# A transformer block: the attention gate applied to finished sums on GpSimd instead of to the output projection's weights, its columns made on VectorE, and the first half's LayerNorm moved to other steps

## The chip, the cores and the metric

The kernel runs on one core of a Trainium2 chip. The core has five engines, which run side by side and meet at semaphores: TensorE (PE in the profile; PEld is its weight load), VectorE (DVE), ScalarE (ACT), GpSimd (POOL) and SyncE (SP, which here only issues DMAs, in the order written). The metric is the device time of one execution in microseconds (us). Three runs of the kernel before took 1762.35, 1762.66 and 1764.65 us; the median is 1762.66 us.

## The reference

The block has 2048 rows of width 512. A condition vector `c` gives six vectors of 512: shift, scale and gate for the attention, and the same for the feed-forward part.

```python
x = A_x
mod = (_silu(c) @ w_mod).reshape(c.shape[0], 6, 1, -1)
sa, ca, ga, sb, cb, gb = (mod[:, 0], mod[:, 1], mod[:, 2], mod[:, 3], mod[:, 4], mod[:, 5])
h = _layernorm(x, axis=-1) * (1 + ca) + sa
x = x + ga * _A_ref(h, A_k_cache, A_v_cache, A_wq, A_wo)
h = _layernorm(x, axis=-1) * (1 + cb) + sb
x = x + gb * _B_ref(h, B_w_gate, B_w_up, B_w_down)
```

`_A_ref` projects `h` with `wq` to 32 query heads of 128, attends for each to 512 cached keys and values (8 key-value heads, four query heads on each), and projects the joined heads with `wo` back to 512. `_B_ref` is `(gelu(h @ w_gate) * (h @ w_up)) @ w_down` with an inner width of 1792. The change concerns `ga`: the gate multiplies the columns of the attention's output, so it may multiply the columns of `wo` beforehand, or the finished sum afterwards.

## The kernel before

**Numbers.** TensorE multiplies 16-bit floats. Every operand is kept as a high and a low half (`t[:, 0]` and `t[:, 1]`, made by `halves`, L152, or `split_post`, L673), and a product is three matmuls (`mm3`, L85 to L88: high by high, high by low, low by high). So that the halves use their range, each weight is multiplied by a scale found from its own sum of squares: ScalarE squares and sums, TensorE adds over partitions, VectorE and GpSimd turn that into a scale and its reciprocal (`norm2`, and the `..._spread` functions).

**Halves and units.** The 2048 rows are 16 tiles of 128. Tiles 0 to 7 are the first half, 8 to 15 the second. In each half, 16 pairs of heads run one after another, and each pair makes four units (two heads by two blocks of 512 rows). A unit is four score tiles; the main loop's counter `t` counts score tiles, 512 in all, and one value of `t` is called a *step* here. In a step TensorE computes one score tile `ps` (three matmuls) and up to three pieces of other work from a queue (query projection, products of probabilities and values `po`, output projection `py`), some 2.6 us in all. VectorE takes the row maximum `nm`, ScalarE the exponential `ee` and the scaled high half of the probabilities `p`, VectorE their low half, and SP issues a transposing DMA of `p` to `pt`. There are two `ps` banks, so the score matmuls of step t+2 wait for the exponential of step t.

**Order.** All order is written by hand. `at(t, f)` puts work behind the pieces of step t, `at(("w", t), f)` behind that, and `at(("d", t), f)` between the maximum and the low half. `sched` lists a load and the steps of its use, and issues the load some steps ahead; `within` issues a load between two steps when SP has no other. Each engine runs its instructions strictly in the order in which they were written. The steps repeat with period 16: even steps hold more VectorE work (a half of a query or output tile, an accumulation) than odd ones.

**Weights.** In the first half every weight is read in 32 bits, scaled, split, used, and stored as halves in `KEPT`; the second half reads them from there. For `wo`, `wo_items` (L570) loads a row tile twice: once for its sum of squares, once to be multiplied, at L584, by a row `gs`, the gate's row times the scale `osc`, and split. `o_spread` (L277) makes `osc` from the sums and `gam`, the greatest absolute value of the gate's row.

**The gate.** Four tiles of `w_mod` are loaded (`gate_load`), and TensorE multiplies them by the activated condition in steps 6 to 9 (`gate_cols`, through `early_cols`, L947), each of the four calls 4 matmuls of 128x128 weights in 32 bits on one column. `mod_row(2)` in step 11 spreads the column over partitions by four transpositions, and ScalarE copies it to `rows[2]`. The other vectors come from `mod_col` (L133): one VectorE instruction, multiply and accumulate, for a tile of `w_mod`.

**Sums.** `acc[ti]` is a row tile's sum in SBUF, of 8 buffers. It is loaded with `x`, and every second pair of heads `y_tasks` (L871) adds a projection result to it (L883). After the last pair `attn_final` (L889) stores it to `y1[ti]` and, three steps later, loads the tile that takes the buffer next.

**LayerNorm.** Rows of the second half's queries are normalised during the first half, two tiles at a time, by `ln_pair` at positions that `plan_pair` takes from `PLAN[1]`; those for the feed-forward part in the second half from `PLAN[2]`. Per pair VectorE has two groups of statistics (L381 to L385) and four wide instructions `xs` (L473, L471), GpSimd four subtractions of half tiles (L479) and four low halves `turn` (L492), ScalarE four high halves, and SP the loads and four transposing DMAs.

**Feed-forward.** Its weights are prepared on GpSimd during the second half (`prep_set`, `prep_wd`; L1341 multiplies a tile of `w_down` by the second gate's row times a scale). After step 512 only matmuls and the gelu remain, product by product: `f_at(q, k, f)` puts work behind product k of set q. The first half's `acc` is reloaded and the second half's rows get their LayerNorm there.

## Time and profile before

The profiled execution took 1763.88 us; its span, first instruction to last, is 1762.1 us.

| what | us |
|---|---|
| median of three runs | 1762.66 |
| profiled execution | 1763.88 |
| its span | 1762.1 |
| TensorE busy | 1724.3 |
| VectorE busy | 1455.9 |
| ScalarE busy | 1207.7 |
| GpSimd busy | 896.2 |
| mean granted TensorE clock | 0.999 of full speed |

Attention runs from about 25 us (step 0) to about 1350 us, the feed-forward part behind it; the first half ends near 690 us. In the rows of a profile L12 is line 12 of the kernel; `a<-b` is a tile written from a tile read, with buffer numbers left out; `x512` counts instructions. A row of groups has the busy time in us and the mean of one instruction in ns, and behind the second bar the engine's idle time before them with the work that ended it. A row of waits has who waited for whom, then total us, times, and the longest. A row of windows has the stretch in us, then busy us and number of instructions for PE, PEld, DVE, ACT and POOL, the granted clock, the share of the DMA engines and GB/s. A row of a timeline has the start and the length in us. Matmuls overlap in the pipeline: one has 379 ns, but they follow each other every 0.216 us.

### The profile page before, as it was taken

How to read it: one execution, taken by the hardware profiler on the slowest of the kernel's cores; microseconds unless marked ns; L12 is line 12 of the kernel's file. 1: busy time of each engine (PE TensorE's matmuls, PEld its weight loads, DVE VectorE, ACT ScalarE, POOL GpSimd, SP SyncE). 2: the span in 40 equal slices, each digit the busy share in tenths (PEclk: the TensorE clock that was granted, in tenths of full speed). 3: DMA queues.
4: the chain of work that ended last, by engine and by line, in shares of the span. 5: the costliest groups of instructions: out<-in, count | busy, mean ns of one | idle time of the engine just before them, and what ended most of it. 6: DMA issues, size and time to landing. Idle time of an engine off the chain costs nothing.

```text
span 1762.1 us, 25746 instructions
## 1 busy us (share of the span) xinstructions
PE 1724.3 (98%) x8034; PEld 787.8 (45%) x8034; DVE 1455.9 (83%) x2541; ACT 1207.7 (69%) x2716; POOL 896.2 (51%) x1113
## 2 busy tenths in 40 slices
PE   8899999999999999999999999999999999999999
PEld 5444444444444444444444444444444444444444
DVE  7888898989898889888888897988875788676666
ACT  6888877777777877778878778788774344434333
POOL 4879878887888773216666667666300233000000
PEclk9999999999999999999999999999999999999999
DMA  7999999999998998999999999999976545252222
GB/s 233 215 195 212 207 213 202 220 199 220 209 213 195 225 203 163 204 214 218 220 214 220 233 223 206 227 224 216 201 143 140 168 127 134 81 200 75 87 75 75
DMA packets 691690, 328.14 MB, mean 186 GB/s; under 512 B 596960, under 2 KB 607456, under 8 KB 691552
## 3 DMA queue, kind: packets, MB, share of 16 engines
q1 hardware_dynamic: 691264, 325.97, 81.0%
q8 instruction: 63, 1.03, 0.2%
q14 instruction: 75, 0.61, 0.1%
q10 hardware_dynamic: 288, 0.52, 0.1%
HBM read 127.54 MB, written 53.61 MB: 103 GB/s over the span
## 4 chain that ended last, share of the span: by engine, by line
PE 77%; POOL 8%; DVE 7%; ACT 4%; issue 2%; DMA 1%; SPq 0%; POOLq 0%; ACTq 0%
PE py L88 8%; PE py L86 8%; PE py L87 8%; PE ps L86 5%; PE ps L88 5%; PE ps L87 5%; PE po L86 5%; PE po L88 5%; PE po L87 5%; PE fa L86 3%; PE fa L88 3%; PE fa L87 3%; PE qa L86 2%; PE qa L88 2%; PE qa L87 2%
## 5 line engine op out<-in xcount | busy, mean ns | idle before, releaser
L915 ACT ACTIVATE ee<-ps,nm 128x512 f32<-128x512 f32 x512 | 350.1, 684 | 265.5 <-DVE nm L906 263.6
L934 DVE SCALAR_TENSOR_TENSOR p<-ee,rr,p 128x512 f16<-128x512 f32 x512 | 452.8, 884 | 1.8 <-ACT p L929 1.5
L906 DVE TENSOR_REDUCE nm<-ps 128x1 f32<-128x512 f32 x512 | 349.9, 683 | 97.3 <-PE ps L88 95.1
L929 ACT ACTIVATE p<-ee,rr 128x512 f16<-128x512 f32 x512 | 363.1, 709 | 8.8 <-DMA pt<-p 8.0
L86 PE MATMUL ps<-k,qt 128*128 128x512 f16 x512 | 193.8, 379 | 20.9 <-ACT ee L915 20.2
L86 PE MATMUL po<-pt,v 128*128 128x512 f16 x512 | 194.1, 379 | 1.6 <-DVE p L934 0.8
L88 PE MATMUL ps<-k,qt 128*128 128x512 f16 x512 | 194.1, 379 | 1.3 <-DVE qt L675 1.3
L87 PE MATMUL py<-wo,ot 128*128 128x512 f16 x512 | 194.0, 379 | 0.0
L88 PE MATMUL py<-wo,ot 128*128 128x512 f16 x512 | 194.0, 379 | 0.0
L88 PE MATMUL po<-pt,v 128*128 128x512 f16 x512 | 194.0, 379 | 0.0
L87 PE MATMUL po<-pt,v 128*128 128x512 f16 x512 | 194.0, 379 | 0.0
L86 PE MATMUL py<-wo,ot 128*128 128x512 f16 x512 | 194.0, 379 | 0.0
L87 PE MATMUL ps<-k,qt 128*128 128x512 f16 x512 | 193.9, 379 | 0.0
L391 POOL TENSOR_TENSOR rs<-rs,nhalf 128x1 f32<-128x1 f32 x32 | 23.4, 731 | 227.4 <-DVE rs L385 224.6
L675 DVE SCALAR_TENSOR_TENSOR ot<-po,ot 128x512 f16<-128x512 f32 x128 | 87.0, 680 | 39.5 <-ACT ot L674 39.3
L87 PEld LDWEIGHTS <-w 128*128 128x128 f16 x728 | 71.3, 98 | 87.0 <-issue 1.7
L88 PEld LDWEIGHTS <-w 128*128 128x128 f16 x728 | 71.3, 98 | 86.6 <-issue 0.8
L86 PEld LDWEIGHTS <-w 128*128 128x128 f16 x728 | 71.2, 98 | 86.7 <-DMA w<-kept 1.3
L883 DVE SCALAR_TENSOR_TENSOR acc<-py,ysc,acc 128x512 f32<-128x512 f32 x128 | 94.5, 738 | 10.9 <-PE py L88 10.9
L883 DVE SCALAR_TENSOR_TENSOR acc<-py,dysc,acc 128x512 f32<-128x512 f32 x112 | 81.3, 744 | 26.4 <-PE py L88 26.2
L915 ACT ACTIVATION_READ_ACCUMULATOR ee<-ps,nm 128x1 f32 x512 | 99.4, 194 | 0.0
L86 PE MATMUL py<-wo,at 128*128 128x512 f16 x224 | 84.9, 379 | 0.0
(269 smaller groups left out, 3760.6 us busy)
## 6 DMA issues: line engine op xcount, KB each, us to landing
w<-kept SPq DMA_DIRECT2D x123, 256.0 KB, 3.3
wo<-kept SPq DMA_DIRECT2D x60, 256.0 KB, 3.5
raw<-in_wo SPq DMA_DIRECT2D x56, 256.0 KB, 3.1
kept<-stage SPq DMA_DIRECT2D x56, 256.0 KB, 3.1
kept<-w SPq DMA_DIRECT2D x39, 256.0 KB, 3.2
rw<-in_wq SPq DMA_DIRECT2D x38, 256.0 KB, 3.2
pt<-p SPq DMA_TRANSPOSE x512, 3.4
kept<-wo SPq DMA_DIRECT2D x32, 256.0 KB, 2.7
```

The source lines that it names most:

```text
L86: nc.tensor.matmul(ps, lhi, rhi, start=first, stop=False, skip_group_check=chain)
L87: nc.tensor.matmul(ps, lhi, rlo, start=False, stop=False, skip_group_check=chain)
L88: nc.tensor.matmul(ps, llo, rhi, start=False, stop=last, skip_group_check=chain)
L391: nc.gpsimd.tensor_tensor(st["rs"], st["rs"], nhalf, op=ALU.pow)
L675: return lambda: nc.vector.scalar_tensor_tensor(t[:, 1, :], src, scale, t[:, 0, :], op0=ALU.mult, op1=ALU.subtract)
L883: nc.vector.scalar_tensor_tensor(acc[ti], st["p"], by, acc[ti], op0=ALU.mult, op1=ALU.add)
L906: nc.vector.tensor_reduce(nm, E[t]["ps"], axis=AX.X, op=ALU.max, negate=True)
L915: nc.scalar.activation(e, E[t]["ps"], AF.Exp, bias=E[t]["nm"], scale=1.0, accum_out=sm[:, t % 2:t % 2 + 1])
L929: nc.scalar.activation(p16[:, 0, :], E[t]["e"], AF.Copy, scale=E[t]["r"])
L934: nc.vector.scalar_tensor_tensor(p16[:, 1, :], E[t]["e"], E[t]["r"], p16[:, 0, :], op0=ALU.mult, op1=ALU.subtract)
```

## The change

The weights of `wo` are multiplied by their scale alone (one GpSimd instruction with a scalar in place of one with two tensors, and no row `gs`). The sum starts afresh from the first projection instead of from `x` (`fresh`), and when it is finished GpSimd multiplies it by the gate's row and adds `x`, which is loaded once more as `xr`. For tiles 0 to 7 this takes place one and three steps after the last accumulation, with the store six steps after; for tiles 8 to 15 at once, with the stores and reloads at listed places of the feed-forward part. The gate's columns come from `mod_col` at steps 207 to 221, its row at step 224. The second gate's row and scale are applied to `w_down` by two instructions per tile, without `gs`. The first two LayerNorm plans become one, a step or two earlier; the third moves six positions later. The `ln` buffers grow from two to three.

```diff
 def mod_row(j):
-        rows[j] = pool.tile([P, D], F32, tag="gate", name="gate", bufs=1)
+        rows[j] = pool.tile([P, D], F32, tag=f"gate{j}", name="gate", bufs=1)
         nc.scalar.activation(rows[j], ps, AF.Copy)
-        absmax(col("gam", j // 3), rows[j])
+        if j == 5:
+            absmax(col("gam", 1), rows[j])
 def o_spread(qd, m):
-        norm2(w, m, 4, 1.0)
-        pool_ts(w, w, col("gam", 0), 1.0 / TOP14)
-        pool_ts(w, w, 1e-30, 1.0, ALU.max)
+        norm2(w, m, 4, 1.0 / TOP14)
...
-            X[k] = pool.tile([P, D], F32, tag="ln", name="xs", bufs=2)
+            X[k] = pool.tile([P, D], F32, tag="ln", name="xs", bufs=3)
...
             def parts(sp=sp, h=h):
-                nc.gpsimd.tensor_tensor(sp["r"], sp["r"], m["g"], op=ALU.mult)
+                times(sp["r"], col("osc", qd))
...
-        def more():
-            m["g"] = pool.tile([P, D], F32, tag="gs", name="gs", bufs=1)
-            pool_ts(m["g"], rows[2], col("osc", qd))
...
+            if fresh:
+                acc[ti] = pool.tile([P, D], F32, tag="acc", name="acc", bufs=2 * QT)
+                ts(acc[ti], st["p"], by)
+            else:
+                nc.vector.scalar_tensor_tensor(acc[ti], st["p"], by, acc[ti], op0=ALU.mult, op1=ALU.add)
...
+    def residual(ti):
+        XR[ti] = pool.tile([P, D], F32, tag="ln", name="xr", bufs=3) if ti < 2 * QT + 3 else raw("xr")
+        dma(XR[ti], rows_of(x, ti))
+    def gate(ti):
+        nc.gpsimd.tensor_tensor(acc[ti], acc[ti], rows[2], op=ALU.mult)
+    def back(ti):
+        nc.gpsimd.tensor_tensor(acc[ti], acc[ti], XR[ti], op=ALU.add)
+    def keep_row(ti):
         y1[ti] = dram.tile([P, D], F32, name=f"y{ti}")
         dma(y1[ti], acc[ti])
-        nxt = (ti + 2 * QT) % NT
-        at(now[0] + 3, lambda: load_acc(nxt, rows_of(x, nxt) if ti < 2 * QT else y1[nxt]))
+    def attn_final(ti):
+        if ti < 2 * QT:
+            residual(ti)
+            at(("w", now[0] + 1), lambda: gate(ti))
+            at(("w", now[0] + 3), lambda: back(ti))
+            at(now[0] + 6, lambda: keep_row(ti))
+        else:
+            gate(ti)
+            back(ti)
...
-    for dt in range(KT):
-        sched(6 + dt, (lambda dt=dt: gate_load(dt), [lambda dt=dt: gate_cols(dt)]), ahead=8)
-    at(("d", 10), lambda: ts(cols[:, 2, :], gps["ps"][:, 0:KT], 1.0, None, ALU.mult))
-    for j, ts_ in ((3, (239, 243, 247, 251)), (4, (241, 245, 249, 253)), (5, (274, 278, 282, 286))):
+    for j, ts_ in ((2, (207, 211, 215, 221)), (3, (239, 243, 247, 251)), (4, (241, 245, 249, 253)), (5, (274, 278, 282, 286))):
...
-    at(11, lambda: mod_row(2))
+    at(224, lambda: mod_row(2))
+    for i in range(2 * QT):
+        at(T - 10 + i, lambda i=i: residual(2 * QT + i))
...
-    PLAN = {1: (-6, 0, 2, 4, -1, 6, 8, 16, 20, 21, ((8, 9, 12), (18, 19, 22), (24, 25, 28), (28, 29, 33))),
-            2: (-6, 0, 2, 5, 8, 14, 16, 18, 21, 22, ((7, 8, 11), (19, 20, 23), (25, 26, 29), (31, 32, 35)))}
+    PLAN = (-6, 0, 2, 4, 0, 6, 10, 16, 19, 20, ((7, 8, 12), (17, 18, 22), (23, 24, 28), (27, 28, 32)))
...
-        plan_pair(1, 78 + 32 * i, i, lambda k, i=i: rows_of(x, 2 * QT + QT * k + i))
-        plan_pair(2, 287 + 48 * i, i, lambda k, i=i: y1[QT * k + i])
+        plan_pair(1, 77 + 32 * i, i, lambda k, i=i: rows_of(x, 2 * QT + QT * k + i))
+        plan_pair(2, 285 + 48 * i, i, lambda k, i=i: y1[QT * k + i])
...
         def make(k):
-            nc.gpsimd.tensor_tensor(st[k], st[k], m["g"], op=ALU.mult)
+            nc.gpsimd.tensor_tensor(st[k], st[k], rows[5], op=ALU.mult)
+            times(st[k], col("dsc", n))
...
-        b = 20 + 16 * i
+        b = 26 + 16 * i
...
+    for i, ((a, b), (c, d)) in enumerate(zip(((1, 3), (1, 3), (1, 4), (1, 5), (2, 0), (2, 1), (2, 3), (2, 5)),
+                                             ((1, 5), (1, 6), (2, 1), (2, 2), (2, 4), (2, 5), (3, 0), (3, 2)))):
+        f_at(a, b, lambda i=i: keep_row(2 * QT + i))
+        f_at(c, d, lambda i=i: load_acc(i, y1[i]))
```

The first place is VectorE in steps 118 to 120 of the first half (a step begins with `nm`; `qt` and `ot` are query and output halves, `p` the probabilities, `xs` a LayerNorm tile). Before:

```order
L906 TENSOR_REDUCE nm<-ps 128x1
L925 RECIPROCAL rr<-rr 128x2
L675 SCALAR_TENSOR_TENSOR qt<-qd,qsc,qt 128x512
L883 SCALAR_TENSOR_TENSOR acc<-py,ysc,acc 128x512
L934 SCALAR_TENSOR_TENSOR p_4235<-ee,rr,p_4235 128x512
L473 SCALAR_TENSOR_TENSOR xs<-xs,mv,row 128x512
L906 TENSOR_REDUCE nm<-ps 128x1
L934 SCALAR_TENSOR_TENSOR p_4263<-ee,rr,p_4263 128x512
L231 TENSOR_REDUCE ysc<-pst 128x1
L906 TENSOR_REDUCE nm<-ps 128x1
```

With the change, the same steps:

```order
L920 TENSOR_REDUCE nm<-ps 128x1
L939 RECIPROCAL rr<-rr 128x2
L665 SCALAR_TENSOR_TENSOR qt<-qd,qsc,qt 128x512
L877 SCALAR_TENSOR_TENSOR acc<-py,ysc,acc 128x512
L948 SCALAR_TENSOR_TENSOR p_4195<-ee,rr,p_4195 128x512
L920 TENSOR_REDUCE nm<-ps 128x1
L948 SCALAR_TENSOR_TENSOR p_4224<-ee,rr,p_4224 128x512
L467 SCALAR_TENSOR_TENSOR xs<-xs,mv,row 128x512
L232 TENSOR_REDUCE ysc<-pst 128x1
L920 TENSOR_REDUCE nm<-ps 128x1
```

The LayerNorm instruction has moved from the end of the even step to the end of the odd one, behind that step's maximum. The pair's other VectorE instructions move in the same way.

The second place is GpSimd around step 130 (`xs` 128x256 are the LayerNorm subtractions; `qsc`, `lr` and `ksc` are scales of queries and keys, `w` and `x` query weights, `vmax` and then `lw` the scale of values, whose reciprocal `vsc` VectorE takes). Before:

```order
L237 TENSOR_SCALAR ksc<-lr,kinv 128x1
L479 TENSOR_TENSOR xs<-xs 128x256 x2
L160 TENSOR_SCALAR rw<-rw,wsc 128x512
L156 TENSOR_SCALAR w_4678<-rw 128x512
L157 TENSOR_TENSOR w_4678<-rw,w_4678 128x512
L479 TENSOR_TENSOR xs<-xs 128x256 x2
L160 TENSOR_SCALAR rw<-rw,wsc 128x512
L156 TENSOR_SCALAR x_4706<-rw 128x256
L157 TENSOR_TENSOR x_4706<-rw,x_4706 128x256
L729 TENSOR_TENSOR rw<-rw 128x256
L233 TENSOR_TENSOR vmax<-vmax,half__86 128x1
```

With the change:

```order
L473 TENSOR_TENSOR xs<-xs 128x256 x4
L238 TENSOR_SCALAR qsc<-lt 128x1
L238 TENSOR_SCALAR lr<-lr,lu 128x1
L238 TENSOR_SCALAR ksc<-lr,kinv 128x1
L161 TENSOR_SCALAR rw<-rw,wsc 128x512
L157 TENSOR_SCALAR w_4634<-rw 128x512
L158 TENSOR_TENSOR w_4634<-rw,w_4634 128x512
L161 TENSOR_SCALAR rw<-rw,wsc 128x512
L157 TENSOR_SCALAR x_4661<-rw 128x256
L158 TENSOR_TENSOR x_4661<-rw,x_4661 128x256
L719 TENSOR_TENSOR rw<-rw 128x256
L234 TENSOR_TENSOR vmax<-vmax,half__86 128x1
```

The four subtractions stand ahead of the scales and weights, and nothing of LayerNorm is left between `ksc` and `vmax`.

More of the change, by code (lines that the diff above doesn't have):

```diff
@@ L286, in second @@
                 y_scale(qd)
-            more()
         then(second)
@@ L304, in d_spread @@
         pool_ts(col("dysc", n), t, 2.0 ** 19, w)
-        def second():
-            nc.vector.reciprocal(col("dsc", n), w)
-            more()
-        then(second)
+        then(lambda: nc.vector.reciprocal(col("dsc", n), w))
     KEPT = {}
@@ L1075, in block_kernel @@
     at(("d", 4), lambda: o1[3][2]())
-    def gate_load(dt):
-        gps[dt] = raw("wmr")
-        dma(gps[dt], wm[1, dt])
-    def gate_cols(dt):
-        if dt == 0:
-            gps["ps"] = bank("qa", "gps", 1)
-        early_cols(gps["ps"], dt, gps[dt])
-    for dt in range(KT):
-        sched(6 + dt, (lambda dt=dt: gate_load(dt), [lambda dt=dt: gate_cols(dt)]), ahead=8)
-    at(("d", 10), lambda: ts(cols[:, 2, :], gps["ps"][:, 0:KT], 1.0, None, ALU.mult))
-    for j, ts_ in ((3, (239, 243, 247, 251)), (4, (241, 245, 249, 253)), (5, (274, 278, 282, 286))):
+    for j, ts_ in ((2, (207, 211, 215, 221)), (3, (239, 243, 247, 251)), (4, (241, 245, 249, 253)), (5, (274, 278, 282, 286))):
         for dt in range(KT):
@@ L1331, in stat @@
             sumsq(m["m"][:, k:k + 1], st[k])
-        def more():
-            m["g"] = pool.tile([P, D], F32, tag="gs", name="gs", bufs=1)
-            pool_ts(m["g"], rows[5], col("dsc", n))
         def spread():
-            d_spread(n, m["m"], more)
+            d_spread(n, m["m"])
         def make(k):
-            nc.gpsimd.tensor_tensor(st[k], st[k], m["g"], op=ALU.mult)
+            nc.gpsimd.tensor_tensor(st[k], st[k], rows[5], op=ALU.mult)
+            times(st[k], col("dsc", n))
             halves(outs[k][0]["t"], st[k])
@@ L1393, in push_y @@
         return [y_tasks(qb * QT + i, [lambda h=h: oT[WHICH[half, h, qb % 2]] for h in hs_], [(half, h) for h in hs_],
-                        col("ysc", qd), attn_final if pr == NPR - 1 else None) for i in range(QT)]
+                        col("ysc", qd), attn_final if pr == NPR - 1 else None, pr == 1) for i in range(QT)]
     ITEMS, hold = {}, [nop]
```

17 lines of the change are left out of this document (8 added, 9 removed).

## The prediction

> **What bounds the kernel now.** I read the page first, then TensorE's waits, then the busy time by stretches, and last the timelines of VectorE and GpSimd around one wait. A *step* is one score tile: three score matmuls `ps`, then VectorE's maximum `nm`, then ScalarE's exponential `ee`, which frees the `ps` bank for the tile two steps on.
>
> ```profile
> span 1762.1 us, 25746 instructions
> PE 1724.3 (98%) x8034; PEld 787.8 (45%) x8034; DVE 1455.9 (83%) x2541; ACT 1207.7 (69%) x2716; POOL 896.2 (51%) x1113
> ...
> PE ps L86 <- ACT ee L915: 20.2, 21, 2.0
> ...
> 60.00:100.00 40.00, 33.60 (x146) 14.10 (x145) 36.18 (x59) 35.71 (x87) 33.10 (x36) 0.96 0.92 203
> ...
> 240.00:560.00 320.00, 304.68 (x1415) 136.44 (x1413) 279.03 (x492) 245.13 (x590) 265.38 (x332) 1.00 0.93 206
> 560.00:700.00 140.00, 139.75 (x654) 63.46 (x653) 122.76 (x231) 106.91 (x252) 89.50 (x108) 1.00 0.93 199
> 700.00:1350.00 650.00, 649.01 (x3030) 294.64 (x3029) 554.99 (x972) 503.34 (x1172) 320.99 (x397) 1.00 0.98 210
> ```
>
> TensorE (first busy column) is the bound, so only two things shorten the kernel: less TensorE work, or less of its 1762.1 - 1724.3 = 37.8 us idle. The idle time sits in few places. From 700 to 1350 us there is 1.0 us, from 560 to 700 us 0.25 us. From 240 to 560 us, where the first half's four LayerNorm pairs run (steps 78 to 206), it is 320 - 304.68 = 15.3 us, and from 60 to 100 us 6.4 us. Both stretches end on the same row: the next score tile waits for ScalarE's `ee`. One such wait, followed back:
>
> ```profile
> 422.38 0.38 PE L86 MATMUL ps<-k,qt 128*128 128x512 f16 x1 [1.91 <-ACT ee L915]
> ...
> 416.44 0.75 DVE L675 SCALAR_TENSOR_TENSOR qt<-qd,qsc,qt 128x512 f16<-128x512 f32 x1 [0.31 <-ACT qt L674]
> ...
> 417.77 1.58 DVE L934 SCALAR_TENSOR_TENSOR p<-ee,rr,p 128x512 f16<-128x512 f32 x1
> 419.28 1.64 DVE L473 SCALAR_TENSOR_TENSOR xs<-xs,mv,row 128x512 f32<-128x512 f32 x1
> 420.84 0.68 DVE L906 TENSOR_REDUCE nm<-ps 128x1 f32<-128x512 f32 x1
> 421.44 0.73 DVE L934 SCALAR_TENSOR_TENSOR p<-ee,rr,p 128x512 f16<-128x512 f32 x1
> ...
> 417.65 1.16 POOL L157 TENSOR_TENSOR w<-rw,w 128x512 f16<-128x512 f32 x1
> 418.77 1.59 POOL L492 TENSOR_TENSOR turn<-xs,turn 128x512 f16<-128x512 f32 x1
> ...
> 421.55 0.69 ACT L915 ACTIVATE ee<-ps,nm 128x512 f32<-128x512 f32 x1 [2.85 <-DVE nm L906]
> ```
>
> ScalarE had been waiting for VectorE. In that even step VectorE has query split, accumulation and probability split, and a LayerNorm instruction comes behind them, ahead of the next maximum. The probability split takes 1.58 us and the LayerNorm instruction 1.64, where the next split, with no GpSimd work beside it, takes 0.73; each of the two ends some 0.55 us after the GpSimd two-input instruction that lies beside it.
>
> **The change part by part.** *LayerNorm slots.* Every VectorE instruction of the first half's pairs leaves an even step with four wide instructions for an odd step with two. That does not shorten VectorE's work. It helps in three ways. First, the maximum of the odd step no longer stands behind a LayerNorm instruction. Second, VectorE's own waits get cover:
>
> ```profile
> DVE vsc L648 <- POOL lw L237: 11.9, 4, 3.1
> ...
> 393.00:422.00 29.00, 26.23 (x122) 11.53 (x120) 25.64 (x47) 21.30 (x53) 23.07 (x30) 1.00 1.03 234
> ...
> DVE qt L675 <- ACT qt L674: 1.1, 2, 0.8
> DVE kinv L248 <- POOL kmax L237: 1.0, 1, 1.0
> DVE ot L675 <- ACT ot L674: 0.8, 1, 0.8
> ...
> L934 DVE SCALAR_TENSOR_TENSOR p<-ee,rr,p 128x512 f16<-128x512 f32 x10 | 8.7, 872 | 0.0
> L473 DVE SCALAR_TENSOR_TENSOR xs<-xs,mv,row 128x512 f32<-128x512 f32 x2 | 2.4, 1190 | 0.0
> L471 DVE SCALAR_TENSOR_TENSOR xs<-xs,rs,row 128x512 f32<-128x512 f32 x1 | 1.6, 1641 | 0.0
> ```
>
> (The first row is VectorE's waits from 240 to 560 us; the others are busy time, waits and groups from 393 to 422 us, the middle of one pair, ten steps.) The waits for `qt` and `ot` are VectorE standing at the head of an even step until ScalarE, released by the odd step's maximum, has made the first half; an instruction in the odd step fills them. Third, the four LayerNorm subtractions on GpSimd (0.73 us each at best) now stand ahead of the key-scale chain instead of between it and the value-scale chain, so that `vsc`, for which VectorE stood 4 times 3 us, comes about 3 us earlier. Bounds of the gain: 0, if the total work and not its order sets the pace, and 15.3 us. The ten steps took 29 us, of which TensorE idled 2.8: it needs 26.2. VectorE was busy 25.6 and waited 2.9 in the rows shown (1.1, 1.0 and 0.8). Stretching is 10 x (0.87 - 0.73) + 2 x (1.19 - 0.73) + (1.64 - 0.73) = 3.2 of its busy time. One group of statistics (one wide instruction, about 0.7, and two small ones, 1.0 by estimate) moves ahead of those steps, I count 2 of the waits as covered and 0.5 of the stretching as gone: 28.5 - 3.5 = 25.0 against 26.2. That fits with 1.2 us of room, but collisions fall where they fall, so I leave 0.8 us to each of four pairs: gain 15.3 - 3.3 = **12.0**.
>
> *Gate columns and output weights, start.* The early TensorE products go:
>
> ```profile
> 44.15 0.95 PE L949 MATMUL gps<-silu,wmr 128*128 128x1 f32 x8
> 44.95 0.38 PE L86 MATMUL ps<-k,qt 128*128 128x512 f16 x1
> ...
> 54.34 0.60 PE L147 MATMUL prow<-ident,cols 128*128 128x128 f32 x4
> 54.77 0.38 PE L86 MATMUL ps<-k,qt 128*128 128x512 f16 x1
> ...
> DVE nm L906 <- PE ps L88: 2.0, 2, 1.7
> DVE gam L189 <- ACT gate L149: 0.6, 1, 0.6
> ```
>
> Four groups at 44.95 - 44.15 = 0.80 are 3.2 us, the transpositions 54.77 - 54.34 = 0.43. In VectorE's waits from 42 to 64 us it stood only 2.0 us for scores, and 0.6 for `gam` ahead of a reduction of about 0.7; beyond these 3.3 us VectorE becomes the bound. So of TensorE's 3.6 us I take 2.5 (bounds 0 and 3.6). Behind it, from 60 to 100 us, VectorE is busy 36.2 of 40 us and GpSimd 33.1, and the clock falls:
>
> ```profile
> 92.00:94.00 2.00, 0.04 (x1) 0.14 (x2) 2.00 (x5) 1.20 (x4) 2.00 (x2) 1.00 0.40 130
> 94.00:96.00 2.00, 2.00 (x7) 0.71 (x7) 2.00 (x3) 1.81 (x5) 2.00 (x2) 0.62 1.01 199
> 96.00:98.00 2.00, 2.00 (x6) 0.72 (x5) 2.00 (x5) 1.97 (x7) 0.18 (x1) 0.52 1.04 116
> ...
> L584 POOL TENSOR_TENSOR raw<-raw,gs 128x512 f32<-128x512 f32 x28 | 43.9, 1568 | 0.5
> L160 POOL TENSOR_SCALAR raw<-raw,vsc 128x512 f32<-128x512 f32 x8 | 6.4, 802 | 0.4 <-DVE vsc L648 0.4
> L584 POOL TENSOR_TENSOR wor<-wor,gs 128x512 f32<-128x512 f32 x4 | 6.1, 1521 | 0.0
> ```
>
> The granted clock of 0.62 and 0.52 costs 2 x (0.38 + 0.48) = 1.7 us, so 6.4 + 1.7 = 8.1 us can be won here. GpSimd loses `gs` (a one-input instruction, 0.8) and 4 x (1.52 - 0.80) = 2.9 us, and two-input instructions that stretch VectorE turn into shorter one-input ones. I take 2.5 (bounds 0 and 8.1; below 0 if the emptied steps let the clock fall, see the rivals). Together **5.0**. The other 28 weight tiles fall by 1.568 - 0.802 = 0.77 us each on GpSimd; that is part of the 12.0.
>
> *Costs.* The row transposition comes back at step 224: 0.43 us. Four gate columns at steps 207 to 221:
>
> ```profile
> L135 DVE SCALAR_TENSOR_TENSOR wmc<-wmc,sbc 128x512 f32<-128x512 f32 x12 | 10.6, 883 | 0.0
> ...
> L492 POOL TENSOR_TENSOR turn<-xs,turn 128x512 f16<-128x512 f32 x12 | 14.1, 1180 | 41.0 <-ACT turn L489 41.0
> ...
> 1373.35 0.75 DVE L883 SCALAR_TENSOR_TENSOR acc<-py,ysc,acc 128x512 f32<-128x512 f32 x1 [1.84 <-PE py L88]
> ...
> 1390.78 1.40 DVE L883 SCALAR_TENSOR_TENSOR acc<-py,dysc,acc 128x512 f32<-128x512 f32 x2
> ```
>
> 4 x 0.88 = 3.5 us beside the 140 - 122.8 = 17.2 us that VectorE idles from 560 to 700 us: 0, or 3.5 without that cover. Gate and residual are 32 new GpSimd instructions. Sixteen fall after 690 us, two per tile, beside at most 18.9 us (16 x 1.18) of locked VectorE; it idles 95 us from 700 to 1350 us, and the steps there have no stall to speak of: 0.5 (bounds 0 and 5). Sixteen come at the attention's end, where the last sums stand 0.75 + 1.84 = 2.59 us apart: 2 x 1.18 = 2.4 us of GpSimd fits between, the last is ready about 1376.5, and the feed-forward adds to the first reloaded tile at 1390.78: 0.5 (0 to 3), since the stores stand ahead of weight loads on SP's queue. The first accumulation without an old value, the added multiplication in the down-projection's preparation (14, less 7 `gs`) and the residual loads lie beside idle VectorE, GpSimd (321 of 650 us busy) and queue: 0. Sum of costs 1.4.
>
> The Trainium skill's page "SBUF — State Buffer", section "SBUF: two separate sides", says that a GpSimd instruction locks VectorE instructions with two SBUF inputs out for its whole length. That speaks against the 32 new instructions, and by it alone all 18.9 us of the first sixteen would be taken from VectorE; the rows at 417 to 420 us agree with the rule.
>
> **Sum.** 12.0 + 5.0 - 1.4 = 15.6 us. The profiled execution took 1763.88 us, 1.8 more than its span, which I keep; so 1748.3 there. The median shown, 1762.66, lies 1.2 below that execution, so the median becomes **1747**.
>
> **Rivals.**
> 1. *Order is not the limit.* VectorE's 28.5 us stays nearly as it is, because the stretching by GpSimd does and the waits only move. For it: GpSimd was busy 265 of 320 us, so an odd step meets its two-input instructions as often. Against: the waits shown have a cause that the new order removes. LayerNorm then gives 4, the start 3: 1762.7 - 7 + 1.4 = 1757. Chance 0.22.
> 2. *Everything clears.* All 15.3 and 8 at the start go, costs 0.5: 1740. For it: 4 x 3 us for `vsc` vanish in any case. Against: only 1.2 us of room. Chance 0.17.
> 3. *Slower: SP's queue stands behind GpSimd.* Each residual load reuses one of three buffers, so it can wait on SP for GpSimd's addition two or three tiles back, and all transpositions of probabilities stand behind it. If GpSimd, waiting for a late weight load, held eight tiles up for a step each, TensorE would lose 8 x 2.59 = 20.7 us: 1768. It decides once a hold outlasts the two units (about 20 us) between a transposition and its use. Against: GpSimd is idle for 31 us at a time there. Chance 0.06.
> 4. *The clock falls early.* With the products gone, steps 6 and 7 leave TensorE 0.65 us of work each against some 1.4 us of VectorE. A fall like that at 94 us costs 1.7 us: 1749. Chance 0.10. The page "TensorE: Matmul & The Clock Gate", section "What's actually happening", asks for an idle window of about 3.4 us; the row here shows a fall behind one gap of 2.0 us.
> 5. *It does not do what it says*: the stalls move to the next heavy step, 1762. Chance 0.05.
>
> Forecast 0.40. A difference under 0.2% (3.5 us) cannot be told from none here. Faster is the forecast, 1, 2 and 4 (0.89), same rival 5 less a little (0.04), slower rival 3 and a little (0.07). The forecast's own range is 1743 to 1752; rivals 1 and 2 widen it to 1739 to 1758.
>
> **What would show it.** Between steps 78 and 206 TensorE's idle time falls from 15.3 to about 3 us, VectorE's wait for `vsc` to under 1 us, and `nm` starts within 3 us of the scores' end. The first 32 steps end some 5 us earlier, without clock 0.5 near 95 us. From 690 to 760 us, and from 1340 to 1400 us, TensorE loses no more than 1 us more than before. The prediction is wrong if TensorE idles over 7 us in the LayerNorm stretch, or if SP's queue shows waits for `acc` from GpSimd with `pt` late behind them.

## The result, and the profile after

The changed kernel takes 1750.03 us (median of six runs, 1749.17 to 1751.18), the kernel before 1762.52 (six runs, 1762.06 to 1764.65): 12.5 us less, a ratio of 0.9927 with a 95% interval of 0.9914 to 0.9940. The forecast was 1747, its own range 1743 to 1752. The profiled execution took 1750.10 us over a span of 1748.3, so the spans differ by 13.8. From the page of the changed kernel:

```profile
span 1748.3 us, 25742 instructions
PE 1718.8 (98%) x8002; PEld 783.7 (45%) x8002; DVE 1469.5 (84%) x2547; ACT 1211.2 (69%) x2716; POOL 918.2 (53%) x1128
```

TensorE is busy 5.5 us less and idles 29.5 us instead of 37.8. Of the 5.5, about 3.2 are the removed products; the rest is how busy time is counted behind a stall, since from step 78 to 206 the same 1511 matmuls count 324.9 us before and 322.2 after. Where the 13.8 us lie is read best from the first score matmul of each step, counted in both traces:

| steps | what happens there | before, us | after, us | difference |
|---|---|---|---|---|
| 0 to 32 | start | 81.2 | 80.2 | -1.0 |
| 32 to 78 | | 117.6 | 117.7 | +0.1 |
| 78 to 206 | the first half's LayerNorm pairs | 340.3 | 323.8 | -16.4 |
| 206 to 272 | gate columns, end of the first half's last pairs | 167.4 | 167.4 | 0 |
| 272 to 304 | first half's gate and residual, start of the second half's LayerNorm | 81.1 | 85.0 | +3.9 |
| 304 to 432 | | 322.8 | 321.9 | -0.9 |
| 432 to 511 | | 198.3 | 198.3 | 0 |
| the rest | begin, feed-forward | | | +0.6 |

So one stretch won more than the whole result, the start next to nothing, and the first half's end gave 3.9 us back. The same places in the busy time by stretches (the columns are those of the prediction's rows: stretch, its length, then PE, PEld, DVE, ACT and POOL busy, the clock, the DMA share):

```profile
60.00:100.00 40.00, 33.39 (x144) 13.90 (x143) 35.04 (x57) 34.60 (x84) 29.02 (x34) 0.96 1.00 207
240.00:560.00 320.00, 318.35 (x1492) 143.95 (x1490) 291.11 (x518) 261.68 (x624) 257.75 (x332) 1.00 1.01 218
560.00:700.00 140.00, 140.00 (x660) 64.39 (x659) 124.86 (x233) 105.99 (x247) 85.69 (x96) 1.00 0.92 202
700.00:1350.00 650.00, 645.52 (x3009) 292.15 (x3008) 556.72 (x959) 494.64 (x1148) 353.63 (x423) 1.00 0.96 209
```

TensorE idles 1.65 us from 240 to 560 us (15.3 before), 6.6 from 60 to 100 us (6.4 before, with the same clock of 0.96), and 4.5 from 700 to 1350 us (1.0 before). VectorE's waits from 240 to 560 us, first one row of the kernel before, then three of the changed kernel:

```profile
DVE ot L675 <- ACT ot L674: 15.4, 20, 0.8
...
DVE nm L920 <- PE ps L88: 16.3, 31, 1.2
DVE ot L665 <- ACT ot L664: 3.1, 4, 0.8
...
DVE vsc L638 <- POOL lw L238: 2.3, 1, 2.3
```

It stood 11.9 us for `vsc` before and 2.3 now, 15.4 for `ot` and 3.1 now, and the largest wait is now that for TensorE's scores, since VectorE is ahead. TensorE's waits from 700 to 1350 us, where before had a single one of 0.8 us:

```profile
PE po L86 <- issue: 1.7, 1, 1.7
PE ps L86 <- ACT ee L929: 1.1, 2, 0.6
PE qa L86 <- ACT u L806: 0.8, 1, 0.8
```

These are the stalls at step 302 (1.7), at 277 and 281 (1.1), and at 289 (0.8). Around the one at step 277, VectorE and then GpSimd in the timeline:

```profile
722.01 1.21 DVE L948 SCALAR_TENSOR_TENSOR p<-ee,rr,p 128x512 f16<-128x512 f32 x1
723.14 1.75 DVE L135 SCALAR_TENSOR_TENSOR wmc<-wmc,sbc 128x512 f32<-128x512 f32 x1
...
722.63 1.72 POOL L890 TENSOR_TENSOR acc<-acc,gate 128x512 f32<-128x512 f32 x1
724.31 1.17 POOL L719 TENSOR_TENSOR rw<-rw 128x256 f32<-128x256 f32 x1
```

The gate's product on GpSimd lies beside a column product of the feed-forward gate on VectorE, which takes 1.75 us, where the twelve before the change took 0.88 in the mean. The gate's product itself takes 1.72.

### The profile page after: what moved, and what is told of

It reads as the page before. It is cut to its first block, busy times and chain, and to the rows that moved or that the text cites. A ratio compares the mean times of both kernels' runs of the same rounds, so it can differ in the third digit from the quotient of the medians.

```text
span 1748.3 us, 25742 instructions
## 1 busy us (share of the span) xinstructions
PE 1718.8 (98%) x8002; PEld 783.7 (45%) x8002; DVE 1469.5 (84%) x2547; ACT 1211.2 (69%) x2716; POOL 918.2 (53%) x1128
## 4 chain that ended last, share of the span: by engine, by line
PE 87%; DVE 5%; POOL 3%; ACT 2%; issue 1%; DMA 1%; SPq 0%; POOLq 0%; ACTq 0%
PE py L88 8%; PE py L86 8%; PE py L87 8%; PE po L88 5%; PE ps L86 5%; PE po L86 5%; PE po L87 5%; PE ps L88 5%; PE ps L87 5%; PE fa L86 3%; PE fa L87 3%; PE fa L88 3%; PE qa L86 3%; PE qa L88 3%; PE qa L87 3%
## 5 line engine op out<-in xcount | busy, mean ns | idle before, releaser
L486 POOL TENSOR_TENSOR turn<-xs,turn 128x512 f16<-128x512 f32 (+1 forms) x48 | 56.6, 1182 | 76.6 <-ACT turn L483 76.3
L890 POOL TENSOR_TENSOR acc<-acc,gate 128x512 f32<-128x512 f32 x16 | 24.2, 1515 | 130.0 <-DVE acc L877 130.0
L877 DVE SCALAR_TENSOR_TENSOR acc<-py,ysc,acc 128x512 f32<-128x512 f32 x112 | 82.7, 738 | 10.9 <-PE py L88 10.9
```

The lines of the kernel that those rows point to most:

```text
L486: nc.gpsimd.tensor_tensor(S[s][:, :, 1, :], side(s), S[s][:, :, 0, :], op=ALU.subtract)
L877: nc.vector.scalar_tensor_tensor(acc[ti], st["p"], by, acc[ti], op0=ALU.mult, op1=ALU.add)
L890: nc.gpsimd.tensor_tensor(acc[ti], acc[ti], rows[2], op=ALU.mult)
```

## Experiments: what made room in the LayerNorm stretch

**Slots alone, weights alone.** `slots` is the kernel before with the new LayerNorm slots of both halves and three `ln` buffers, and nothing else; `oldslots` is the changed kernel with the old ones in the first half; `heavywo` gives each tile of the output weights a two-input GpSimd product again:

```diff
 # heavywo, on the changed kernel
-                times(sp["r"], col("osc", qd))
+                nc.gpsimd.tensor_tensor(sp["r"], sp["r"], col("osc", qd).to_broadcast([P, D]), op=ALU.mult)
 # oldslots, on the changed kernel, with the old table for the first half as well
 # (slots is the reverse for both halves, on the kernel before)
-        plan_pair(1, 77 + 32 * i, i, lambda k, i=i: rows_of(x, 2 * QT + QT * k + i))
+        plan_pair(1, 78 + 32 * i, i, lambda k, i=i: rows_of(x, 2 * QT + QT * k + i))
```

> The kernel before with the new LayerNorm slots alone (the new table, pairs from steps 77 and 285, three buffers). Theory, the order sets the pace: TensorE's idle time from 240 to 560 us falls from 15.3 to under 4 us with the old two-input weight products still there, 1749 to 1751 us. Rival, the lighter GpSimd work of the weights made the room (28 x 0.77 = 21.6 us of GpSimd): the slots alone win at most 6 us, 1756 or more, and 9 us or more of the idle time stay.

> The changed kernel with the first half's LayerNorm pairs back in the old slots (from step 78). Theory, order: at least 10 of the 15.3 us idle between steps 78 and 206 return, 1760 to 1764 us. Rival, lighter GpSimd: at most 6 us return, 1756 or less.

> The changed kernel with each of the 32 weight tiles multiplied by its scale in a two-input GpSimd instruction again (the scale's column read as a 128x512 operand), so GpSimd is about 0.77 us longer for each. Theory, order: the LayerNorm stretch stays without stall (idle under 4 us between steps 78 and 206) and the time within 2 us of 1750. Rival, lighter GpSimd: 6 us or more of stalls come back there, 1756 or more. For the start, four of these lie before step 25: if VectorE's locks by the weights set the stalls at steps 24 and 28, step 32 starts 1 us or more later than the changed kernel's 105.1 us; if not, within 0.4 us of it.

Measured: 1753.63 us for `slots`, 1763.30 for `oldslots`, 1752.87 for `heavywo`. Steps 78 to 206 take 325.9, 336.8 and 325.1 us, with 3.3, 13.0 and 2.4 us in TensorE's stalls. The stretch from 240 to 560 us in `slots`:

```profile
240.00:560.00 320.00, 316.73 (x1482) 142.99 (x1481) 292.25 (x510) 259.86 (x617) 275.31 (x341) 1.00 1.01 217
```

So the order did it, with GpSimd's heavy products still there. These cost 1.3 to 2.1 us of the stretch with the new order (325.1 and 325.9 against 323.8); with the old order, the lighter products win 3.5 us (340.3 to 336.8). `heavywo` kept its stretch as expected, but came out 2.8 us above the changed kernel instead of within 2. At the start, its steps 16 to 28 take 31.9 us against 30.7 in the changed kernel; by step 32 it is 0.6 us later, because the clock falls behind step 28 in the changed kernel and not in `heavywo`. So the lighter products are worth some 1 us at the start as well. `slots` came out 2.6 us above the expectation for a reason that lies elsewhere: step 302, below. And `oldslots` says something about the change as a whole: all of it but the first half's slots is worth nothing (ratio to before 1.0002, interval 0.9993 to 1.0012). What the start and the lighter weights win (0.9 and 3.5 us in its profile), the first half's end (3.7) and the time outside the steps (1.0) take back.

**Which of the moved numbers.** The new table differs from the old in four ways, and the prediction gave three reasons without a price for each: odd steps, covered waits, earlier subtractions. Four runs take them apart, all on the changed kernel:

```diff
 # even: one step later, same table
-        plan_pair(1, 77 + 32 * i, i, lambda k, i=i: rows_of(x, 2 * QT + QT * k + i))
+        plan_pair(1, 78 + 32 * i, i, lambda k, i=i: rows_of(x, 2 * QT + QT * k + i))
 # a1old: even, and the second tile's first scaling at its old step (86, 118, ...)
-(-6, 0, 2, 4, 0, 6, 10, 16, 19, 20, ((7, 8, 12), (17, 18, 22), (23, 24, 28), (27, 28, 32)))
+(-6, 0, 2, 4, 0, 6,  8, 16, 19, 20, ((7, 8, 12), (17, 18, 22), (23, 24, 28), (27, 28, 32)))
 # sides: a1old, and the work on the four sides a step later, at its old steps
+(-6, 0, 2, 4, 0, 6,  8, 16, 19, 20, ((8, 9, 12), (18, 19, 22), (24, 25, 28), (28, 29, 33)))
 # subsold: the changed kernel, GpSimd's four subtractions two steps later, at their old steps
+(-6, 0, 2, 4, 0, 6, 10, 16, 21, 22, ((7, 8, 12), (17, 18, 22), (23, 24, 28), (27, 28, 32)))
```

> The changed kernel with the first half's LayerNorm pairs one step later (from step 78): the same spacing, GpSimd's lighter weights and its subtractions still ahead of the key-scale chain by one step less, but every VectorE instruction of LayerNorm behind the four wide ones of an even step again. Theory, the odd steps are what counts: 8 us or more of the 15.3 us of idle time return between steps 78 and 206, 1757 or more. Rival, the spacing and the earlier subtractions (value scale 3 us earlier) count: at most 4 us return, 1754 or less.

> The first half's LayerNorm pairs from step 78 with the new table, of which the run before this one showed that it stalls hardly at all (2.1 us between steps 78 and 206), and one number of it back as before: the first scaling of the second tile two steps earlier, at step 86 and every 32 steps, on the step after GpSimd's residue of the first side. Theory, the crowding of that one place made the stalls of 1.6 to 1.9 us ahead of steps 89, 121, 153 and 185 (the maximum of step 151 began 4.92 us after its scores in the old slots, 2.45 in the new table from 78): they come back, 6 us or more, 1757 or more. Rival, the other numbers (GpSimd's subtractions and sides a step earlier): at most 2 us come back, 1753 or less.

> The changed kernel with GpSimd's four LayerNorm subtractions of each pair at their old steps (98 and 99 and every 32) instead of 96 and 97; all else stays. Theory: VectorE's wait for the value scale grows from 2.3 to about 12 us (3 us in each pair), yet costs only the 0.45 us ahead of steps 105, 137 and 169 and something at 200, 2 us or less in all: 1750 to 1752. Rival, the forecast's third reason as a main part of the 12 us: 4 us or more of stalls return, 1754 or more.

> The run with the second tile's first scaling at its old step (4 stalls of 0.45 us), and GpSimd's and ScalarE's work on the four sides of each pair one step later as before; GpSimd's four subtractions stay a step earlier (97, 98) than in the old slots. In the old slots GpSimd's residue of the first side comes straight behind the residue of a query weight (1.16 and 1.59 us), and VectorE's split of p and the scaling take 1.58 and 1.64 us beside them; with the sides a step earlier the residue goes first, and they take 0.94 and 1.09. Theory, VectorE's lock by two two-input GpSimd instructions in a row: the stalls ahead of steps 89, 121, 153 and 185 grow from 0.45 to 1.6 us or more, 4.5 us or more in all come back on top of 1752.6, 1757 or more. Rival, GpSimd's subtractions at 98 and 99 are the rest of the old slots' loss: under 2 us come back, 1754.5 or less.

| run | median, us | steps 78 to 206, us | in TensorE's stalls there, us |
|---|---|---|---|
| before | 1762.52 | 340.3 | 15.3 |
| oldslots (lighter weights) | 1763.30 | 336.8 | 13.0 |
| sides (+ subtractions a step earlier) | 1757.40 | 330.6 | 7.8 |
| a1old (+ sides a step earlier) | 1752.60 | 326.8 | 3.8 |
| even (+ scaling two steps later) | 1751.28 | 324.6 | 2.1 |
| the changed kernel (+ odd steps) | 1750.03 | 323.8 | 1.7 |
| subsold (the changed kernel, subtractions back) | 1756.24 | 329.6 | 5.9 |

Read downwards, the 16.4 us are 3.5 for the lighter weights, 6.2 for the subtractions (with one load a step later), 3.8 for the sides, 2.2 for the scaling and 0.8 for the odd steps. Taken away in another order, the parts would differ, as `slots` and `heavywo` showed for the weights. The stretch is the better measure: the six profiles with the changed kernel's weights and slots there (itself, `nogate`, `cols5`, `gen2`, `tlate11`, `best2`) take 323.8 to 324.2 us in it, while the medians come from several sessions, in which the kernel before took from 1762.5 to 1763.7. The odd steps, my first reason and my expectation for `even`, count for almost nothing. The scaling was the theory for `a1old`, with 6 us, and fell too: it brought back four stalls of 0.45 us. The third reason, GpSimd's subtractions, is the largest, though I had expected 2 us at most by then: `subsold` loses 5.8 us in the stretch. Put back late, they hold up not only VectorE but TensorE, as its waits from 240 to 560 us in `subsold` show:

```profile
PE po L88 <- POOL v L158: 3.4, 4, 0.9
PE ps L86 <- ACT ee L929: 1.9, 4, 0.6
```

In GpSimd's order the value scale and the split of `v` stand behind the subtractions, and so they are late for the product that needs `v`.

What the sides do (GpSimd's low halves and ScalarE's high halves move together) is seen at step 151, the place that the prediction followed back. In `sides`, VectorE and then GpSimd:

```profile
410.94 1.59 DVE L948 SCALAR_TENSOR_TENSOR p<-ee,rr,p 128x512 f16<-128x512 f32 x1
412.45 1.64 DVE L467 SCALAR_TENSOR_TENSOR xs<-xs,mv,row 128x512 f32<-128x512 f32 x1
...
410.82 1.16 POOL L158 TENSOR_TENSOR w<-rw,w 128x512 f16<-128x512 f32 x1
411.94 1.60 POOL L486 TENSOR_TENSOR turn<-xs,turn 128x512 f16<-128x512 f32 x1
```

The same place in `a1old`:

```profile
409.14 0.94 DVE L948 SCALAR_TENSOR_TENSOR p<-ee,rr,p 128x512 f16<-128x512 f32 x1
410.01 1.09 DVE L467 SCALAR_TENSOR_TENSOR xs<-xs,mv,row 128x512 f32<-128x512 f32 x1
...
408.38 1.16 POOL L486 TENSOR_TENSOR turn<-xs,turn 128x512 f16<-128x512 f32 x1
409.51 1.05 POOL L157 TENSOR_SCALAR w<-rw 128x512 f16<-128x512 f32 x1
```

In `sides` GpSimd runs two two-input instructions in a row, each beside one of VectorE's, which take 3.2 us together. In `a1old` the side's residue comes first, a one-input instruction stands next, and VectorE needs 2.0. The stalls are 1.63 us in the one and 0.45 in the other, four times. The Trainium skill, page "SBUF — State Buffer", section "SBUF: two separate sides", says that whichever engine starts first holds the pair of ports for its whole instruction; the rows agree, since GpSimd's residue begins at 411.94 while the split of `p` runs until 412.53, and takes 1.60 us instead of 1.16. The busy times from step 78 to 206, in the kernel before:

```profile
223.66:563.91 340.25, 324.93 (x1511) 145.66 (x1510) 296.95 (x527) 261.01 (x629) 277.80 (x349) 1.00 0.93 207
```

and in the changed kernel:

```profile
222.79:546.61 323.82, 322.17 (x1511) 145.72 (x1509) 296.19 (x529) 265.01 (x631) 261.83 (x336) 1.00 1.01 219
```

VectorE is busy 297.0 us and 296.2: its work did not shrink, it lies elsewhere.

## Experiments: the start

```diff
 # tlate11: three of GpSimd's four subtractions that make T move from steps 25 and 26 to 30 and later
-combos(p, nc.gpsimd if p == 0 else nc.vector, 1 if p else 2, 0 if p else 5)
+combos(p, nc.gpsimd if p == 0 else nc.vector, 1 if p else 2, 0 if p else 11)
```

> The changed kernel with three of the four GpSimd subtractions that make T (1.6 us each, two inputs, 85 to 91 us in the profile) moved behind step 28, past 99 us, where GpSimd idles for 8.8 us. Theory, the start's last large stall (2.23 us ahead of step 28) is VectorE locked out by these, not by the weights' products that the change made shorter: k's and p's splits of 1.57 and 1.64 us fall to about 0.75, the stall to 0.7 us or less, and step 32 starts at 103.3 us or earlier against 105.1. Rival, what sets the pace there is the transposed probabilities coming late behind VectorE's whole work: step 32 gains under 0.6 us, and the wait turns up as one of the po products for pt.

Measured: 1757.82 us, so the run lost 7.8 us, yet its first half went as the theory said. The splits of `k` and `p` that took 1.57 and 1.64 us take 0.75 and 0.74, and the stall ahead of step 28 falls from 2.23 to 0.42 us. So the stall at step 28 comes from these subtractions, which the change does not touch, and not from the weights' products (2.26 us in `heavywo`); the one at step 24 (1.9 us) stays. But the gain stopped there: the next product waits 1.79 us for its transposed probabilities, and step 32 comes only 0.9 us earlier. Then SP's queue stands, as its largest wait and TensorE's waits from 85 to 125 us show:

```profile
SPq L94 <- POOL T L369: 7.9, 1, 7.9
...
PE po L86 <- DMA pt<-p: 7.3, 2, 5.5
PE ps L86 <- ACT ee L929: 0.4, 1, 0.4
```

A load that reuses a buffer read by the last subtraction waits 7.9 us at the head of SP's queue, the transpositions behind it are late, TensorE stands 5.5 us, and the clock falls to 0.50 behind it. I had not listed that wait.

The other half of the start's term, TensorE's removed products, is answered by the first score matmuls: step 16 comes 1.9 us earlier, but the twelve steps behind it take 1.0 us longer (30.7 against 29.7), with the stalls ahead of steps 24 and 28 grown from 1.6 and 2.0 to 1.9 and 2.2 us, and by step 32 it is 0.9. In `slots`, where the start is as before, step 32 comes 1.1 us earlier than in the kernel before, 0.7 of it because there the clock did not fall behind the stall at step 28. Of the starts without a fall of the clock behind step 28, the old one (`slots`) takes 80.5 us to step 32, the new one with heavy weights (`heavywo`) 80.9, and the whole new one 79.7 to 80.1 in seven runs: by these, what is left of the gain at step 32 comes from the lighter weights. So the start's part of the change is worth about 1 us, and the clock alone makes runs differ by up to 0.7.

## Experiments: the first half's end and the second half's LayerNorm

```diff
 # nogate: the first half's gate and residual left out
-            at(("w", now[0] + 1), lambda: gate(ti))
-            at(("w", now[0] + 3), lambda: back(ti))
 # cols5
-(5, (274, 278, 282, 286))
+(5, (258, 262, 266, 270))
 # gen2
-        plan_pair(2, 285 + 48 * i, i, lambda k, i=i: y1[QT * k + i])
+        plan_pair(2, 287 + 48 * i, i, lambda k, i=i: y1[QT * k + i])
 # best2: columns at (264, 266, 268, 270), and the second half's pairs by the old table from 287
```

> The changed kernel without the 16 GpSimd instructions that multiply by the gate and add x for the first half (that half's gate and residual are left out). The changed kernel loses 3.9 us against the one before between steps 272 and 304. Theory, these instructions are the cause, by the lock (stalls of 0.56, 0.53 and 0.82 us at steps 277 to 289) and by GpSimd's lateness, for which a load on SP's queue waits ahead of a transposition (1.68 us at step 302): all four stalls go, 1746 to 1747. Rival, the second half's earlier LayerNorm slots (two steps) and the transposition of B that stands one place earlier on SP's queue: the 1.68 us stay and at most 2 us return, 1748 to 1750.

> The changed kernel with the four column products of the feed-forward gate on VectorE at steps 258, 262, 266 and 270 instead of 274, 278, 282 and 286, where GpSimd's gate and residual of the first half begin. Theory, the pile-up of both in one place: a column product takes 1.75 us beside a gate product and 0.88 without; the stalls at steps 277, 281 and 289 (1.91 us together) fall to 0.5 or less, 1748 to 1748.8. Rival, gate and residual alone lock out VectorE's splits and sums: 1.3 us or more of the stalls stay.

> The changed kernel with the second half's LayerNorm pairs two steps later (from 287, 335, 383 and 431; the first transposition of B then stands behind two more transpositions of probabilities on SP's queue). From the runs so far: step 302 takes 2.81 us before, 4.43 with the whole change, 6.64 with the slots alone and 4.03 without the first half's gate. Theory, SP's queue: B's transposition ahead of that of the probabilities is the cause; step 302 takes at most 3.0 us, 1748 to 1748.6. Rival, the wait of a load on SP for GpSimd's staged tile (3.1 us, 2.3 before) is the cause: step 302 keeps 4 us or more, time unchanged at 1750.

> The changed kernel with the second half's LayerNorm pairs in their old slots (old table, from step 287) and the feed-forward gate's columns at steps 264, 266, 268 and 270, where the maximum follows its scores by 0.04 us and ScalarE is 2.9 us ahead. Theory, both losses of the second half come from places on the clock of the steps, not from the gate's and the residual's work itself: steps 277 to 289 without stall, step 302 at 3 us or less instead of 4.43, 3 to 3.5 us less in all, 1746.5 to 1747.5. Rival, as in the runs that moved these pairs and the columns one at a time: each move sets up a new late place on SP's queue or VectorE, and the time stays at 1749 to 1751.

| run | median, us | steps 272 to 304, us | stalls from step 276 to 290, us | step 302, us |
|---|---|---|---|---|
| before | 1762.52 | 81.1 | 0 | 2.81 |
| the changed kernel | 1750.03 | 85.0 | 1.9 | 4.43 |
| nogate | 1748.88 | 82.4 | 0 | 4.03 |
| slots | 1753.63 | 85.1 | 0 | 6.64 |
| cols5 | 1750.11 | 81.9 | 0 | 3.74 |
| gen2 | 1756.10 | 85.5 | 1.0 | 4.70 |
| best2 | 1748.02 | 80.8 | 0 | 2.59 |

Two mechanisms, then. The stalls at steps 277 to 289 need both parts, gate products and column products: they vanish without the gate (`nogate`) and with the columns elsewhere (`cols5`). They are not the same in each run: the eight profiles that leave this place as the changed kernel has it hold 1.0 to 1.9 us of them and take 83.8 to 86.2 us over the steps, all more than `nogate` and `cols5`. `cols5` is no gain on balance, because TensorE now stands 1.11 us at step 261, between the first two of its columns, and 0.86 at step 398.

Step 302 is not the gate's doing: it stays in `nogate`, and is worst in `slots`, which has no gate there (some 5.1 us of its 6.64 are the stall and the work, the rest a lower clock, see the last section). On SP's queue in the changed kernel, with the late product behind it (`<-issue`: the profile names no work that released it):

```profile
785.31 0.34 SPq L94 DMA_DIRECT2D rw<-in_wu  x1
785.70 0.42 SPq L94 DMA_DIRECT2D kept<-stage  x1
786.22 1.45 SPq L952 DMA_TRANSPOSE pt<-p  x1
787.71 1.31 SPq L490 DMA_TRANSPOSE B<-turn  x1
789.12 0.74 SPq L94 DMA_DIRECT2D rw<-in_wu  x1
789.91 0.62 SPq L94 DMA_DIRECT2D kept<-stage  x1
790.64 1.27 SPq L952 DMA_TRANSPOSE pt<-p  x1
...
794.43 0.38 PE L86 MATMUL po<-pt,v 128*128 128x512 f16 x1 [1.68 <-issue]
```

The issues of the same place, from 770 to 796 us (count, median us from issue to landing):

```profile
pt<-p SPq DMA_TRANSPOSE x10, 3.6
```

The load at 785.31 waited 3.1 us for GpSimd's staged tile (2.3 us in the kernel before), and then `B`'s transposition, which stood one place later before, goes ahead of that of the probabilities. Issued at 790.64, they land at 794.34 by the trace, 3.7 us later, and the product, which TensorE was free to begin at 792.75, follows at 794.43. The expectation for `gen2` was that later slots cure this. They put `B` two places back, and made two other late places instead: 0.5 and 1.9 us at step 302, 2.5 us at step 410; the median is 6.1 us worse. The theory about the queue's order was too simple; what the runs show is that of the three orders tried only the old one holds this spot near the 2.6 us of a step (2.81 us before, 2.59 in `best2`).

`best2` puts the second half's pairs back where they were and moves the columns to steps where the maximum follows its scores at once. Steps 272 to 304 take 80.8 us, so the whole 3.9 us of loss is gone with gate and residual still on GpSimd. It takes 1748.02 us (five runs, 1747.11 to 1748.83), 2 us less than the changed kernel, where I had expected 3 to 3.5; small stalls at steps 410 and 466 (0.57 and 0.36) and 0.4 us in the feed-forward part take some of it back. Its ratio to the kernel before is 0.9915 (0.9901 to 0.9928). That interval overlaps the changed kernel's, but the slowest of its runs lies below the fastest of those, although the kernel before took 1763.51 us in its session and 1762.52 in the other.

## Why the prediction was right, and where it was not

The time came out 3 us above the forecast, within its own range, and by the mechanism on which it rested most: the order of the LayerNorm work, not its amount, set the pace. The reason that it gave first for this, the odd steps, was not the one that counted. And two terms were off by about 4 us each, in opposite directions, so that the total came out so near is in part luck. Of the 3 us, 1.8 are the sum (13.8 against 15.6); the other 1.2 were taken off because the profiled execution before stood above the median, and the one after stands on it.

- **LayerNorm slots, 12.0 (bounds 0 to 15.3): 16.4.** The step that failed is "I leave 0.8 us to each of four pairs" (four times 0.8 is 3.2, where 3.3 was taken off): hardly anything was left, TensorE's idle time from 240 to 560 us falling by 13.7 to 1.65; the other 2.8 us are busy time counted behind the stalls, which the bound of 15.3 did not hold. That order sets the pace was right, and the term too small. Of the three reasons, the odd steps are worth 0.8, and the subtractions, which I put last, 6.2. The sides on GpSimd (3.8) I had not seen, though the quoted rows showed both instructions.
- **Start, 5.0: 0.9.** The sentence that failed is the one that gave 2.5 to the stretch from 60 to 100 us because GpSimd becomes lighter there. The rows that stretch VectorE at steps 25 to 28 are GpSimd's four subtractions for T, untouched by the change. I took the sum of GpSimd's work instead of looking which instruction lay beside the late split. And the 1.7 us counted for the clock were not to be had in full: with the clock full, the next product waits for its probabilities (1.07 us in `nogate`), so that four steps take 11.6 us instead of 12.1. Of the 2.5 set for TensorE's removed products, 1.9 had come by step 16 and were lost again by step 32; the lighter weights gave some 1 us (`heavywo`).
- **Costs, 1.4: 3.6.** Row transposition, gate columns and attention's end cost nothing that shows (steps 206 to 272 are equal to 0.1 us; the 60 us around the attention's end, from 1340 us before and 1326 after, hold 0.69 us of idle time in both). The first half's end was set at 0.5 of a range to 5, and took 3.9, less 0.9 won at step 414; 0.6 more lies outside the steps, mostly in the feed-forward part. A gate product was priced at 1.18 us, the mean of another instruction, and takes 1.70 to 1.72 in the first half. The argument that failed is that "the steps there have no stall to speak of": that they did not stall said nothing of how much more they could take. And a part of it is a term that the sum lacks: the second half's LayerNorm slots were moved as well, and I costed them at nothing without saying so.
- **Rivals.** "Order is not the limit" is refuted by `slots`, and by the two rows of VectorE's equal busy time over stretches that differ by 16.4 us. "Everything clears" was right of the LayerNorm stretch and wrong of the rest. The slower rival's mechanism exists: SP's queue did stand behind GpSimd, in the changed kernel at step 302 (through a staged tile and `B`, not through the residual loads), and in `tlate11`. Its trigger was far off: a hold of 7.9 us, not of 20, was enough to stop TensorE for 5.5. The clock did not fall in the emptied steps 6 and 7.
- **What was to show it.** The idle time and, in all but one pair, the wait for `vsc` came as written; `nm` lags its scores by 3.3 and 4.0 us in two of 128 steps, by less than 3 in all others. That the first 32 steps end 5 us earlier, and without the low clock near 95 us, did not come, and from 690 to 760 us TensorE idled 1.9 us (0.0 before) instead of at most 1 more; from 700 to 1350 us it idled 3.5 more.

## What to carry to other kernels

Where two engines share the pace, busy times say little: list what one has beside, and ahead of, the other's late step, and move one of the two. Two shifts by one step, of GpSimd's subtractions and of the sides' work on GpSimd and ScalarE, were worth 10 of the 16.4 us here, at equal busy time of VectorE. A stretch without stalls may still be full, so read the slack (from the scores' end to the maximum, from the exponential's end to the next scores) before putting anything there, and look at what a load at the head of an in-order queue waits for and what stands behind it.

## What was not expected of the hardware

The granted clock does not follow the length of the gap alone. Behind a stall of 2.23 us in the changed kernel it falls to half for 3.4 us, behind 2.25 us in `nogate` not at all. The traces' own records of the clock show what decides. In all fourteen, each such fall begins a whole number of 3.413 us after the first record of the clock and lasts 3.413 us, or twice that in `tlate11`. In the changed kernel the first record stands at 18.63 us and the fall at 93.72, which is 22 times 3.413 later. Cut at these times, the changed kernel, and then `nogate`, whose first record stands at 19.87 us (the clock is the third number from the end):

```profile
90.31:93.72 3.41, 1.18 (x7) 0.42 (x6) 3.41 (x6) 2.31 (x6) 0.73 (x1) 1.00 0.58 155
93.72:97.13 3.41, 3.41 (x10) 1.21 (x9) 3.18 (x6) 3.38 (x10) 0.00 (x0) 0.50 1.23 194
97.13:100.54 3.41, 3.41 (x17) 1.55 (x16) 1.35 (x2) 2.59 (x8) 0.73 (x1) 1.00 1.00 297
```

```profile
88.14:91.55 3.41, 3.04 (x15) 1.19 (x13) 2.90 (x3) 3.32 (x9) 3.27 (x3) 1.00 1.14 159
91.55:94.96 3.41, 1.53 (x8) 0.79 (x9) 3.41 (x7) 2.37 (x6) 0.00 (x0) 1.00 0.79 194
94.96:98.37 3.41, 2.51 (x12) 0.95 (x10) 2.92 (x6) 3.38 (x11) 0.00 (x0) 1.00 0.98 251
```

The same stall lies whole in one stretch of the changed kernel, where TensorE idles 2.23 us, and is shared between two in `nogate`, where it idles 0.37 and 1.88. Over the some 500 such stretches of each trace, half clock follows all 15 in which TensorE idled 2.00 us or more, and none in which it idled 1.94 or less. (The last 5 us of each trace are left out; two idle times of 1.99 and 2.01 us there were not followed by a fall.) The Trainium skill, page "TensorE: Matmul & The Clock Gate", section "What's actually happening", puts the half clock behind an idle window of about 3.4 us; here 2.0 us of idle time within such a window was enough. Its 3.4 us at half clock agree with the row: 3.41 x 0.50 = 1.7 us of lost clock in the changed kernel.

In `slots` the clock falls behind 2.50 us at step 302 and makes that step 6.64 us long, where the stall alone would have made it some 5.1. At the start it costs little: from step 28 to 32 the changed kernel takes 12.07 us with the fall, `nogate` 11.61 without, since the time won goes into a wait of 1.07 us for the transposed probabilities.
